# A convolution operand loaded ready-made from four masked copies in HBM, in place of GpSimd copies on chip

## The chip, the cores and the metric

The kernel runs on one core of a Trainium2 chip. The metric is the device time of one execution in microseconds. The core's engines are TensorE (PE; its weight loads are listed as PEld), VectorE (DVE), ScalarE (ACT), GpSimd (POOL) and SyncE (SP), which here issues nearly all DMAs from one queue in order.

## The reference

Two independent computations fill the two halves of one output of 2048 x 1280 (bf16). S is 2048 and D is 640.

```python
# A: gated long convolution
k_shift = sum over t of k_pad[:, t:t+S, :] * shift_k[:, 3-t]     # 4 taps
kv  = k_shift * v
y   = irfft(rfft(kv padded to 2S) * rfft(ssm_k padded to 2S))[:S]  # causal conv per channel
a   = q * (y + kv * ssm_D)
# B: attention with 32 heads of 20
q, k, v = split(x @ wqkv)
b   = softmax(q @ k.T * 20**-0.5) @ v  -> merged heads @ wo
out = concatenate([a, b], axis=-1)
```

The exponentials of B are 32 x 2048 x 2048, which is 2048 tiles of 128 x 512.

## The kernel before

**B.** For each of 4 query chunks of 512, 8 groups of 4 heads and 16 key blocks of 128, four score matmuls (L559) write PSUM banks. ACT takes them two or three banks at a time through Exp into `P_sb` (L576). Some tiles go to DVE instead: a bit-trick exponential in five steps, L606 (reads PSUM), L609, L611, L614 and L616 (writes `P_sb`), in slots of their own. L637 multiplies `P_sb` with V and accumulates over the key blocks in one bank. The casts of K, Q, V and of the results are on DVE. When PE has nothing to do, `zeros` (L314) issues matmuls with a zero operand.

**A, kv stage.** `kv_iter` (L469) builds kv on DVE, 16 blocks of 128 time steps: four products with the taps, three sums, one product with v, each a `tensor_tensor` over 128 x 640 (L472). Each block is stored twice from SP: to `kv_scratch` in order, and to `kvr_scratch` with each run of 32 rows reversed. Two input buffers (`kst`) are loaded two blocks ahead.

**A, convolution.** The causal convolution is a product with Toeplitz tiles. Four channels share one matmul over 128 partitions, each in 32 of them. `hk_load` (L827) brings, for each quad of channels, overlapping rows of the filter from `kext_scratch` into one of four `HK` buffers: four DMAs of 132 KB. The other operand must be block-diagonal: of the four columns of a quad, column X is nonzero only in partitions 32X to 32X+31. `kvr_load` brings half of the channels into `KVr`; `kvx_build` (L833) spreads eight quads of it into one of two `KVX` buffers by four POOL copies of 32 x 512 (L839). The zeros in `KVX` come from two memsets at the start (L816). Inside a `KVX` buffer the 64 columns that a matmul reads are contiguous. `conv_iter` issues 32 matmuls per quad (L871, 8 to 128 columns), for 160 quads; after four quads (16 channels) DVE splits a half of the result into high and low parts (L884, L885), four matmuls add it shifted (L892), and L898 copies the 16 channels into `Y`.

**A, output.** When 20 such groups of 16 channels, thus 320 channels, are done, `A_iter` runs: per block of 128 time steps three DVE steps of 128 x 320 (L914), loads of q and kv and a store (L925) on SP.

**The order** of everything is made while the program is built. A list planner (`Prog`, and the loop from L1078) keeps an estimated time for each engine, with given costs `c` and a DMA estimate of 215 KB per us (L149), and emits each instruction into its engine's fixed stream. It gives ACT its next tiles first; it places conv matmuls and casts in the PE slack that remains; kv and A steps are `micro` work that fills DVE gaps. `vec_at` (L1062) decides whether one more tile goes to DVE: not while kv is behind `(now - 60) * KVPACE` steps, and not while the running `A_iter` is behind its pace of 48 steps per 240 us, or per 60 us once the conv is over. Semaphore waits follow from the buffers (`Buf`); on the chip each engine runs its stream in that order whatever the real times are.

```python
def kvx_build(c):
    B, cl = divmod(c, 10)
    i = c % 2
    for X in range(4):
        dst = sub(KVX[i], [[256, 8], [64, 4], [4, 16]], X, 32 * X, 32)
        src = sub(KVr, [[1, 8], [80, 4], [320, 16]], cl * 8, 32 * X, 32)
```

Of the kernel before, what the change touches and what calls it, by code (L numbers as in the profile page):

```python
# [6 lines left out]
ALU = mybir.AluOpType  # L7
# [4 lines left out]
S = 2048  # L12
D = 640
# [11 lines left out]
NHK = 4  # L25
NPA, NPV = 25, 4
# [4 lines left out]
KVPACE, CONV0, CONVE = 1.0, 560, 40  # L31
# [179 lines left out]
def build_kernel(nc, A_q, A_k, A_v, A_shift_k, A_ssm_k, A_ssm_D, B_x, B_wqkv, B_wo, out):  # L211
# [3 lines left out]
    with ExitStack() as es:  # L215
# [21 lines left out]
        XZ_sb = sb("XZ", [128, 2, 512], FP32)  # L237
# [3 lines left out]
        ident = sb("ident", [128, 128])  # L241
        Win = sb("Win", [128, 128])
        Wc = sb("Wc", [128, 128])
# [3 lines left out]
        HK_E, KVR_E, KVX_E, Y_E, AST_E = HKW, 64 * 80, 8 * 256, 16 * 320, 320  # L247
        ph0 = NCC * 2 * D + 4 * 4 * D + 2 * 5 * D + KS * D + 2 * D + 2 * D
        ph1 = NHK * HK_E + KVR_E + 2 * KVX_E + 2 * Y_E + 5 * AST_E
# [5 lines left out]
        def carve(n):  # L255
# [8 lines left out]
        tA, tB = carve(D), carve(D)  # L264
        kvst = [carve(D) for _ in range(2)]
        pos[0] = 0
        HK = [carve(HK_E) for _ in range(NHK)]
        KVr = carve(KVR_E).rearrange("p (j c) -> p j c", j=64)
        KVX = [carve(KVX_E) for _ in range(2)]
        Y = [carve(Y_E).rearrange("p (t c) -> p t c", t=16) for _ in range(2)]  # L270
        Aq = [carve(AST_E) for _ in range(3)]
        Akv = [carve(AST_E) for _ in range(2)]
# [9 lines left out]
        kvr_d = nc.dram_tensor("kvr_scratch", (S, D), BF16).ap()  # L282

        b_ident, b_Win, b_Wc, b_ones, b_tA, b_tB, b_C = (Buf() for _ in range(7))
# [5 lines left out]
        b_XI, b_XZ = [Buf(), Buf()], [Buf(), Buf()]  # L290
# [10 lines left out]
        b_kvd, b_kext, b_kshT = [], Buf(), Buf()  # L301


        P.op("pool", lambda e: e.memset(ident, 0.0), writes=[b_ident])
        P.op("pool", lambda e: e.affine_select(out=ident, in_=ident, compare_op=ALU.not_equal, fill=1.0, base=0,
                                               pattern=[[-1, 128]], channel_multiplier=1),
# [150 lines left out]
        d_kvr, d_sk, d_kext, d_small = DS("kvr"), DS("sk"), DS("kext"), DS("small")  # L457
# [11 lines left out]
        def kv_iter():  # L469

            def mul(o, a, b, op, reads, writes):
                P.op("dve", lambda e: e.tensor_tensor(o, a, b, op), reads=reads, writes=writes, c=0.49)  # L472

            for j in range(KS):
                src = ap(kst[1], [list(kst[1].ap[0]), [KS, D]], KS - 1 - j)
                yield [b_kst[1]]
                P.op("dve", lambda e, j=j, src=src: e.tensor_copy(Ctile[:, j, :], src), reads=[b_kst[1]], writes=[b_C],
                     c=0.49)
            kst_load(1)
            for tb in range(NKB):  # L480
                i = tb % 2
                k = kst[i]
                yield [b_kst[i]]
                mul(tA, k[:, 0, :], Ctile[:, 0, :], ALU.mult, [b_kst[i], b_C], [b_tA])
                for j in range(1, KS):
                    yield []
                    mul(tB, k[:, j, :], Ctile[:, j, :], ALU.mult, [b_kst[i], b_C], [b_tB])
                    yield []
                    mul(tA, tA, tB, ALU.add, [b_tA, b_tB], [b_tA])
                yield b_kvst[i].r and [RB(b_kvst[i])]  # L490
                mul(kvst[i], tA, k[:, KS, :], ALU.mult, [b_kst[i], b_tA], [b_kvst[i]])
                bd = Buf()
                P.dmas("sp", [(kvd[tb * 128:(tb + 1) * 128, :], kvst[i]),
                              (ap(kvr_d, [[32 * D, 4], [-D, 32], [1, D]], (tb * 128 + 31) * D), kvst[i])], d_kvst[i],
                       reads=[b_kvst[i]], writes=[bd])
                b_kvd.append(bd)
                if tb + 2 < NKB:
                    kst_load(tb + 2)

        def setup_pool():  # L500
            P.op("pool", lambda e: e.memset(V_sb[:, :, :, DH:DH + 1], 1.0), writes=[b_ones])
            for t in (Win, Wc):
                bb = b_Win if t is Win else b_Wc
                P.op("pool", lambda e, t=t: e.memset(t, 0.0), writes=[bb])
                base = 32 if t is Win else -96
                P.op("pool", lambda e, t=t, base=base: e.affine_select(
                    out=t, in_=t, compare_op=ALU.not_equal, fill=1.0, base=base,
                    pattern=[[-1, 128]], channel_multiplier=1), reads=[bb], writes=[bb])
            P.op("pool", lambda e: e.memset(kst[0][0:KS - 1, 0:KS, :], 0.0), writes=[b_kst[0]])
            P.op("pool", lambda e: e.memset(tB, 0.0), writes=[b_tB])  # L510
# [80 lines left out]
        def vexp_iter(n, bk):  # L591
# [4 lines left out]
            XI, XZ, bi, bz = XI_sb[:, i, :], XZ_sb[:, i, :], b_XI[i], b_XZ[i]  # L596
# [206 lines left out]
        d_aq = [DS("aq%d" % i) for i in range(3)]  # L803
        d_ao = [DS("ao%d" % i) for i in range(3)]

        def conv_setup():
            allx = [b_WK0, b_WQ0, b_Wa, b_Wb] + b_x0 + b_xst + b_kst + [b_C, b_tA, b_tB] + b_kvst
            cv["HK"] = [Buf(*allx) for _ in range(NHK)]
            cv["KVr"] = Buf(*allx)
            cv["KVX"] = [Buf(*allx) for _ in range(2)]  # L810
            cv["Y"] = [Buf(*allx) for _ in range(2)]
            cv["Aq"] = [Buf(*allx) for _ in range(3)]
            cv["Akv"] = [Buf(*allx) for _ in range(2)]
            cv["Z"] = [Buf(), Buf()]
            for i in range(2):
                P.op("pool", lambda e, i=i: e.memset(KVX[i], 0.0), writes=[cv["KVX"][i]], c=1.9)  # L816
            kvr_load(0)
            for qd in range(NHK):
                hk_load(qd)
            kvx_build(0)  # L820
            kvx_build(1)

        def kvr_load(B):
            P.dmas("sp", [(KVr[32 * X:32 * X + 32], ap(kvr_d, [[D, 32], [32 * D, 64], [1, 80]], 320 * B + 80 * X))
                          for X in range(4)], d_kvr, reads=b_kvd, writes=[cv["KVr"]])

        def hk_load(qd):  # L827
            B, m = divmod(qd, 80)
            P.dmas("sp", [(HK[qd % NHK][32 * X:32 * X + 32],
                           ap(kext, [[1, 32], [1, HKW]], (320 * B + 80 * X + m) * KXL + 1)) for X in range(4)],  # L830
                   d_hk[qd % NHK], reads=[b_kext], writes=[cv["HK"][qd % NHK]])

        def kvx_build(c):  # L833
            B, cl = divmod(c, 10)
            i = c % 2
            for X in range(4):
                dst = sub(KVX[i], [[256, 8], [64, 4], [4, 16]], X, 32 * X, 32)
                src = sub(KVr, [[1, 8], [80, 4], [320, 16]], cl * 8, 32 * X, 32)
                P.op("pool", lambda e, dst=dst, src=src: e.tensor_copy(dst, src), reads=[cv["KVr"]],  # L839
                     writes=[cv["KVX"][i]] if X == 3 else [], extra=(cv["KVX"][i].r + cv["KVX"][i].w) if X == 0 else (), c=1.35)  # L840
            if cl == 9 and B == 0:
                kvr_load(1)

        def conv_reads(bt):
            rd = []
            for qd in range(4 * bt, 4 * bt + 2):
                rd += [cv["HK"][qd % NHK], cv["KVX"][(qd // 8) % 2]]
            return rd

        def conv_iter():  # L850

            for bt in range(40):
                B, j = divmod(bt, 20)
                for u in range(4):
                    conv_at[0] = u
                    qd = bt * 4 + u
                    c, ql = divmod(qd, 8)
                    i = c % 2
                    slot = qd % NHK
                    for d in range(16):  # L860
                        for r1 in range(2):
# [4 lines left out]
                            rhs = sub(KVX[i], [[64, 2], [1, n]], ql * 256 + r1 * 128)  # L866
# [3 lines left out]
                            yield (cost, [cv["HK"][slot], cv["KVX"][i]] if first else [])  # L870
                            P.op("pe", lambda e, o=o, lhsT=lhsT, rhs=rhs, st=st, last=last: e.matmul(  # L871
                                o, lhsT, rhs, start=st, stop=last, skip_group_check=True),
                                reads=[cv["HK"][slot], cv["KVX"][i]], writes=[bkb[MISC]], tok=last, c=cost,
                                st=0.8 * cost)
                            if last:
                                if qd + NHK < 160:
                                    hk_load(qd + NHK)
                                if ql == 7 and c + 2 < 20:
                                    kvx_build(c + 2)
# [15 lines left out]
                P.op("pe", pe, reads=[bz[0], bz[1], b_Win, b_Wc], writes=[bkb[MISC]], c=0.43, st=0.42)  # L895
# [349 lines left out]
```

## Time and profile before

| What | Value |
|---|---|
| median of 6 runs | 923.43 us (921.43 to 935.74) |
| profiled execution | 925.29 us, span 923.5 us |
| ACT busy | 890.5 us (96%) |
| PE busy | 883.6 us (96%), of which L314 106.7 |
| DVE busy | 631.1 us (68%) |
| POOL busy | 128.0 us (14%) |
| mean granted TensorE clock | 0.985 |
| tiles whose exponential is on DVE (L606) | 110 of 2048 |
| DMA packets | 82015, 129.18 MB |

A row of the groups gives line, engine, operation, tiles, shapes and count, then busy time and mean duration, then the engine's idle time just before and what ended it. In the slices, the span is cut into 40 equal parts of 23.1 us and a digit is the busy share in tenths. PE's ends are modelled, so its busy time is not a measure of how full it is.

### The profile page before, as it was taken

The page shows a single profiled execution, that of the slowest core. Times are in us where ns is not written, and L with a number is a line of the kernel's source. Part 1 is how long each engine was busy: PE and PEld are TensorE (multiplying, and loading weights), DVE is VectorE, ACT ScalarE, POOL GpSimd, SP SyncE. Part 2 cuts the span into 40 slices and gives each one's busy share as a digit, 9 for nine tenths or more (in the row PEclk, how much of TensorE's full clock was granted, in tenths as well). Part 3 has the DMA queues.
Part 4 walks back from the last instruction along what each step waited for, and adds up shares of the span by engine and source line. Part 5 has one row for each costly group of instructions (what it writes and reads, how often), then busy time and mean ns, then how long its engine had stood idle before and what let it go on. Part 6 is the DMA issues. An engine that isn't in the chain of part 4 may idle for free.

```text
span 923.5 us, 26598 instructions
## 1 busy us (share of the span) xinstructions
PE 883.6 (96%) x11742; PEld 413.1 (45%) x11742; DVE 631.1 (68%) x1166; ACT 890.5 (96%) x787; POOL 128.0 (14%) x97
## 2 busy tenths in 40 slices
PE   9999998998988999999999999999999999999998
PEld 5443322223644555555445555555555555422222
DVE  4467666668776777877777778777777776744651
ACT  7999999999997999999999999999999999999995
POOL 3000000006202202222022201222210220000000
PEclk9999999999997999999999999999999999999997
DMA  9421334529644565765586666675675766222000
GB/s 289 160 87 52 124 127 146 165 71 176 170 114 126 150 172 130 188 164 146 146 159 169 162 178 188 173 200 156 173 200 143 188 175 176 70 72 72 12 1 29
DMA packets 82015, 129.18 MB, mean 140 GB/s; under 512 B 32977, under 2 KB 58699, under 8 KB 81899
## 3 DMA queue, kind: packets, MB, share of 16 engines
q1 hardware_dynamic: 79739, 124.36, 49.8%
q0 software_dynamic: 704, 2.74, 0.9%
q8 instruction: 92, 1.51, 0.7%
q10 hardware_dynamic: 1456, 0.37, 0.2%
q14 instruction: 24, 0.20, 0.1%
HBM read 116.81 MB, written 13.23 MB: 141 GB/s over the span
## 4 chain that ended last, share of the span: by engine, by line
PE 52%; ACT 41%; DVE 6%; DMA 1%; issue 0%; SPq 0%; DVEq 0%
ACT P_sb L576 41%; PE PS L871 18%; PE PS L559 14%; PE PS L637 9%; PE PS L389 3%; PE PS L314 2%; PE PS L892 2%; PE PS L711 2%; DVE P_sb L616 2%; DMA R<-in_B_x_dram 1%; DVE XI L614 1%; PE PS L661 1%; DVE XZ L609 1%; PE PS L694 0%; PE PS L740 0%; DVE XZ L611 0%
## 5 line engine op out<-in xcount | busy, mean ns | idle before, releaser
L576 ACT ACTIVATE P_sb<-PS 128x1024 bf16<-128x1024 f32 (+1 forms) x779 | 886.0, 1296 | 19.4 <-PE PS L559 17.5
L559 PE MATMUL PS<-QT,KT 20*128 20x512 bf16 x2048 | 304.7, 388 | 21.4 <-ACT P_sb L576 19.8
L871 PE MATMUL PS<-R 128*128 128x128 bf16 (+15 forms) x5120 | 242.0, 194 | 1.1 <-DVE R L898 0.6
L871 PEld LDWEIGHTS PS<-R 128*128 128x128 bf16 x5120 | 197.9, 97 | 93.4 <-issue 92.9
L839 POOL COPY R<-R 32x512 bf16<-32x512 bf16 x80 | 115.6, 1445 | 423.7 <-PE PS L871 413.6
L559 PEld LDWEIGHTS PS<-QT,KT 20*128 20x128 bf16 x2048 | 74.4, 91 | 218.8 <-ACT P_sb L576 151.0
L637 PE MATMUL PS<-P_sb,V_sb 128*21 128x512 bf16 x2048 | 162.3, 391 | 10.1 <-DVE P_sb L616 10.0
L606 DVE TENSOR_SCALAR XI<-PS 128x512 int32<-128x512 f32 x110 | 76.0, 691 | 110.9 <-PE PS L559 110.5
L314 PE MATMUL PS<-Zt 128*128 128x512 bf16 x358 | 106.7, 393 | 1.0 <-DVE Zt L308 1.0
L616 DVE SCALAR_TENSOR_TENSOR P_sb<-XZ,XI 128x512 uint16<-128x512 f32 x110 | 83.3, 757 | 2.2
L609 DVE SCALAR_TENSOR_TENSOR XZ<-XI 128x512 f32<-128x512 uint16 x110 | 80.5, 732 | 1.2
L611 DVE SCALAR_TENSOR_TENSOR XZ<-XZ,XI 128x512 f32<-128x512 f32 x110 | 79.5, 723 | 2.2
L637 PEld LDWEIGHTS PS<-P_sb,V_sb 128*21 128x21 bf16 x2048 | 33.0, 90 | 73.4 <-issue 48.9
L472 DVE TENSOR_TENSOR R<-R 128x640 bf16<-128x640 bf16 x128 | 61.2, 488 | 5.2 <-DMA R<-in_A_v_dram 1.9
L614 DVE TENSOR_SCALAR XI<-XI 128x512 int16<-128x512 int16 x110 | 58.7, 534 | 2.4
L646 DVE CAST OT_sb<-PS 128x512 bf16<-128x512 f32 x32 | 22.0, 688 | 37.3 <-PE PS L637 37.0
L314 PEld LDWEIGHTS PS<-Zt 128*128 128x128 bf16 x358 | 23.9, 98 | 40.3 <-issue 33.1
L389 PE MATMUL PS<-xT,R 128*20 128x512 bf16 (+2 forms) x660 | 40.4, 374 | 0.0
L389 PE MATMUL PS<-xT,WQ 128*20 128x512 bf16 (+1 forms) x660 | 40.2, 374 | 0.0
L377 DVE CAST KT<-PS 128x512 bf16<-128x512 f32 (+1 forms) x32 | 21.7, 679 | 26.2 <-PE PS L389 26.2
L450 DVE CAST V_sb<-PS 128x160 bf16<-128x160 f32 (+1 forms) x48 | 18.4, 382 | 21.6 <-PE PS L444 20.8
L377 DVE CAST QT<-PS 128x512 bf16<-128x512 f32 (+1 forms) x32 | 21.9, 683 | 16.0 <-PE PS L389 15.7
(56 smaller groups left out, 354.9 us busy)
## 6 DMA issues: line engine op xcount, KB each, us to landing
R<-kext_scratch SPq DMA_DIRECT2D x640, 132.0 KB, 3.0
R<-in_A_k_dram SPq DMA_DIRECT2D x15, 640.0 KB, 3.9
kext_scratch<-in_A_ssm_k_dram POOLq DMA_DIRECT2D x1, 2560.0 KB, 14.3
R<-in_A_v_dram SPq DMA_DIRECT2D x16, 160.0 KB, 5.4
kv_scratch<-R SPq DMA_DIRECT2D x16, 160.0 KB
kvr_scratch<-R SPq DMA_DIRECT2D x16, 160.0 KB
R<-kvr_scratch SPq DMA_DIRECT2D x8, 320.0 KB, 6.5
R<-in_A_q_dram SPq DMA_DIRECT2D x32, 80.0 KB, 2.2
```

Of the source, the lines that this page charges most:

```text
L314: P.op("pe", lambda e: e.matmul(bank[bk], Zt, zrhs, start=start, stop=start, skip_group_check=True), reads=[b_Zt], writes=[bkb[bk]], tok=s ...
L389: ins = e.matmul(bank[bk][32 * i:32 * i + DH, 0:n], Wt[:, cc, off + i * DH:off + (i + 1) * DH], xT[:, cc, x0:x0 + n], start=(cc == 0), sto ...
L559: ins = e.matmul(bank[b], KT[32 * u:32 * u + DH, g, kb * 128:(kb + 1) * 128], QT[32 * u:32 * u + DH, qs(qc, g), :], start=True, stop=True, ...
L576: P.op("act", lambda e: e.activation(P_sb[:, s0:s0 + k, :], PS[:, b0 * 512:(b0 + k) * 512].rearrange("p (u q) -> p u q", u=k), ACT.Exp, sc ...
L606: step(lambda e: e.tensor_scalar(XI, bank[bk], scale * 1.4426950408889634 * w, 127.0 * w, op0=ALU.mult, op1=ALU.add), [bkb[bk]], [bi])
L609: step(lambda e: e.scalar_tensor_tensor(XZ, u, w * c2 / c3, u, op0=ALU.add, op1=ALU.mult), [bi], [bz])
L611: step(lambda e: e.scalar_tensor_tensor(XZ, XZ, w * w * c1 / c3, u, op0=ALU.add, op1=ALU.mult), [bi, bz], [bz])
L614: step(lambda e: e.tensor_scalar(hi, hi, 128.0, None, op0=ALU.mult), [bi], [bi])
L616: step(lambda e: e.scalar_tensor_tensor(P_sb[:, slot[n], :].bitcast(U16), XZ, 128.0 * c3 / w ** 3, hi, op0=ALU.mult, op1=ALU.add), [bi, bz ...
L637: ins = e.matmul(bank[OBANK][32 * u:32 * u + DH + 1, :], V_sb[:, kb, 4 * g + u, :], P_sb[:, slot[4 * b + u], :], start=(kb == 0), stop=(kb ...
L839: P.op("pool", lambda e, dst=dst, src=src: e.tensor_copy(dst, src), reads=[cv["KVr"]], writes=[cv["KVX"][i]] if X == 3 else [], extra=(cv[ ...
L871: P.op("pe", lambda e, o=o, lhsT=lhsT, rhs=rhs, st=st, last=last: e.matmul(o, lhsT, rhs, start=st, stop=last, skip_group_check=True), read ...
```

## The change

`kv_iter` computes two taps in one instruction and stores kv in order once. In addition DVE copies each kv block into one of two tiles `KM`, at every fifth group of positions, such that copy X of the four in a tile holds only the channels with index X modulo 4 and is zero elsewhere. Four DMAs per block store these to `kvm_scratch`, each run of 32 rows reversed. `KVr`, the POOL copies and the memsets of `KVX` are gone; two DVE memsets clear `KM`. `kvx_load` brings 128 channels at once into `KVX`, one DMA for each X, in pieces of 128 channels (256 B); the next chunk's four loads are issued after each of the first four groups of 16 channels of the present one. The matmuls (before L871) read their columns from `KVX` at a step of 128 channels per 32 time steps, four adjacent elements at a time. `A_iter` runs five times, once per 128 channels, in four steps of 512 time steps, with two `Aq` buffers instead of three. Its pace becomes 12 steps per 60 us, or per 20 us once the conv is over; KVPACE becomes 0.9. The second exponential path has one `XZ` buffer instead of two. `ident`, `Win` and `Wc` become windows of one tile. The `HK` buffers wait only for what lay in their own memory.

```diff
+CH = 128
-KVPACE, CONV0, CONVE = 1.0, 560, 40
+KVPACE, CONV0, CONVE = 0.9, 560, 40
...
-        XZ_sb = sb("XZ", [128, 2, 512], FP32)
+        XZ = sb("XZ", [128, 512], FP32)
...
+            for i in range(2):
+                yield [RB(b_xst[2 + i])]
+                b_KM.append(Buf(b_xst[2 + i]))
+                P.op("dve", lambda e, i=i: e.memset(KM[i], 0.0), writes=[b_KM[i]], c=0.8)
...
-                yield [b_kst[i]]
-                mul(tA, k[:, 0, :], Ctile[:, 0, :], ALU.mult, [b_kst[i], b_C], [b_tA])
+                for j in range(0, KS, 2):
+                    yield [b_kst[i]]
+                    mul(tB[:, j:j + 2, :], k[:, j:j + 2, :], Ctile[:, j:j + 2, :], ALU.mult, [b_kst[i], b_C], [b_tB], 0.82)
                 for j in range(1, KS):
                     yield []
-                    mul(tB, k[:, j, :], Ctile[:, j, :], ALU.mult, [b_kst[i], b_C], [b_tB])
-                    yield []
-                    mul(tA, tA, tB, ALU.add, [b_tA, b_tB], [b_tA])
+                    mul(tA, tA if j > 1 else tB[:, 0, :], tB[:, j, :], ALU.add, [b_tA, b_tB], [b_tA])
...
-                P.dmas("sp", [(kvd[tb * 128:(tb + 1) * 128, :], kvst[i]),
-                              (ap(kvr_d, [[32 * D, 4], [-D, 32], [1, D]], (tb * 128 + 31) * D), kvst[i])], d_kvst[i],
-                       reads=[b_kvst[i]], writes=[bd])
                 if tb + 2 < NKB:
                     kst_load(tb + 2)
+                P.dma("sp", kvd[tb * 128:(tb + 1) * 128, :], kvst[i], d_kvst[i], reads=[b_kvst[i]], writes=[bd])
+                yield b_KM[i].r and [RB(b_KM[i])]
+                P.op("dve", lambda e, i=i: e.tensor_copy(sub(KM[i], [[D + 1, 4], [4, D // 4]]),
+                                                         sub(kvst[i], [[1, 4], [4, D // 4]])),
+                     reads=[b_kvst[i]], writes=[b_KM[i]], c=0.73)
+                P.dmas("sp", [(ap(kvm_d, [[32 * D, 4], [-D, 32], [1, D]], (X * S + tb * 128 + 31) * D),
+                               KM[i][:, X * D:(X + 1) * D]) for X in range(4)], d_km[i], reads=[b_KM[i]], writes=[bm])
...
-            for i in range(2):
-                P.op("pool", lambda e, i=i: e.memset(KVX[i], 0.0), writes=[cv["KVX"][i]], c=1.9)
-            kvr_load(0)
-            for qd in range(NHK):
+            hk_load(0)
+            for X in range(4):
+                kvx_load(0, X)
+            for qd in range(1, NHK):
                 hk_load(qd)
-            kvx_build(0)
-            kvx_build(1)
...
+        def kvx_load(c, X):
+            P.dma("sp", KVX[c % 2][32 * X:32 * X + 32].rearrange("p (j c) -> p j c", j=64),
+                  ap(kvm_d, [[D, 32], [32 * D, 64], [1, CH]], X * S * D + CH * c), d_kvx[c % 2][X],
+                  reads=b_kvm, writes=[cv["KVX"][c % 2][X]])
...
-                            rhs = sub(KVX[i], [[64, 2], [1, n]], ql * 256 + r1 * 128)
+                            rhs = sub(KVX[i], [[CH, 2], [4 * CH, 16 - d], [1, 4]], r1 * 2 * CH + 4 * ql)
...
-                                if ql == 7 and c + 2 < 20:
-                                    kvx_build(c + 2)
+                                if u == 3 and j < 4 and c + 1 < D // CH:
+                                    kvx_load(c + 1, j)
...
-            for tp in range(16):
+            for h in range(4):
...
-                P.dma("sp", ap(out2, [[2 * D, 128], [1, 320]], tp * 128 * 2 * D + 320 * B), Aq[i], d_ao[i], reads=[q])
+                P.dma("sp", ap(out2, [[2 * D, 128], [128 * 2 * D, 4], [1, CH]], h * 512 * 2 * D + CH * B), Aq[i],
+                      d_ao[i], reads=[q])
...
-            elif micro and kv_done[0] < a_at[0] + 48 * (now - a_at[1]) / (60 if conv_over else 240):
+            elif micro and kv_done[0] < a_at[0] + 12 * (now - a_at[1]) / (20 if conv_over else 60):
```

## The prediction

> **What bounds the kernel.** I read the slices first, then the groups, then busy times by stage, then the waits of the convolution stage, and last the timeline of one disturbed place. From the slices, ScalarE (ACT), GpSimd (POOL) and the granted TensorE clock:
>
> ```profile
> ACT  7999999999997999999999999999999999999995
> POOL 3000000006202202222022201222210220000000
> PEclk9999999999997999999999999999999999999997
> ```
>
> ACT is full nearly everywhere; the one hole inside the run (slice 13, 277 to 300 us) has POOL at work and a lowered clock. ACT does the exponentials (L576: 575.4 + 432.3 us in the two shapes), so the time is ACT's work plus ACT's idle time. By stage (columns: stretch, length, PE, PEld, DVE, ACT, POOL busy with counts, clock, DMA share, GB/s):
>
> ```profile
> 60.00:208.00 148.00, 138.14 (x1447) 43.77 (x1444) 98.27 (x199) 147.91 (x132) 0.00 (x0) 1.00 0.35 114
> 208.00:320.00 112.00, 103.61 (x1435) 52.80 (x1432) 82.80 (x135) 102.66 (x90) 29.93 (x20) 0.92 0.62 149
> 320.00:440.00 120.00, 117.55 (x1843) 64.83 (x1844) 91.83 (x153) 118.35 (x105) 26.24 (x19) 1.00 0.59 159
> 440.00:560.00 120.00, 117.25 (x1778) 63.02 (x1774) 90.08 (x161) 119.31 (x106) 23.03 (x16) 1.00 0.65 163
> 560.00:680.00 120.00, 119.21 (x1897) 65.26 (x1893) 91.64 (x168) 119.53 (x106) 23.17 (x16) 1.00 0.67 179
> 680.00:800.00 120.00, 118.46 (x1857) 66.26 (x1853) 88.37 (x162) 118.21 (x103) 17.03 (x12) 1.00 0.63 166
> ```
>
> Before 208 us ACT idles 0.09 us in 148. From 208 to 800 us it works 102.66 + 118.35 + 119.31 + 119.53 + 118.21 = 578.06 of 592 us: 13.9 us idle, and POOL works only there. The waits of 208 to 800 us (total, times, longest) and one place of the timeline (start, length) show the path:
>
> ```profile
> PEld PS L559 <- ACT P_sb L576: 48.2, 122, 0.8
> PEld PS L637 <- DVE P_sb L616: 15.9, 21, 2.7
> ACT P_sb L576 <- PE PS L559: 12.3, 18, 2.1
> ```
>
> ```profile
> 284.72 3.32 POOL L839 COPY R<-R 32x512 bf16<-32x512 bf16 x2
> ...
> 285.40 1.47 DVE L614 TENSOR_SCALAR XI<-XI 128x512 int16<-128x512 int16 x1
> ...
> 286.90 1.45 DVE L616 SCALAR_TENSOR_TENSOR P_sb<-XZ,XI 128x512 uint16<-128x512 f32 x1
> ...
> 288.40 0.61 PE L637 MATMUL PS<-P_sb,V_sb 128*21 128x512 bf16 x4 [2.44 <-DVE P_sb L616]
> ...
> 289.60 2.36 ACT L576 ACTIVATE P_sb<-PS 128x1536 bf16<-128x1536 f32 x2 [2.07 <-PE PS L559]
> ```
>
> While a POOL copy runs, VectorE (DVE) steps of the second exponential path stretch: L614 takes 1.47 us where its median is 0.458, L616 1.45 where it is 0.691. L637, fixed in PE's order, waits 2.44 us, the next scores come late, ACT idles 2.07. L606, which reads PSUM, never exceeds 0.694 us.
>
> **Removed.** L839's 80 copies of 1445 ns (115.6 us) and L816's two memsets (3.8 us) leave POOL. POOL bounds nothing; what counts is ACT's idle time behind them. Mean over median times 110 gives the DVE time lost beside the copies: L609 5.3, L611 3.5, L614 8.4, L616 7.3, together 24.4 us, reaching ACT as at most 13.9. Some is ordinary PE jitter: I take the 12.3 us of ACT waits less what lies outside copies, **-12.0** (0 to -13.9; the lower end if another wait stands right behind).
>
> **The kv stage on DVE.** L472 costs 488 ns at 640 elements, L914 326 ns at 320: 0.506 ns an element, so a double-width product (1280) costs 0.812 us. After: 32 x 0.812 + 48 x 0.488 + 16 x 0.488 = 57.2 us, where L472 has 61.2. The masked copy (640 elements at step 4) has a near row, L477, a copy reading at step 4: 0.497 us. Bounds 0.5 and 1.0; I take 0.6, 9.6 us for 16. Two memsets, about 2. Sum +7.6 us. The 50 us in which DVE idles from 60 to 208 us hide it; without this cover kv ends 8 us later, the conv starts later and about two DVE exponentials are lost. One moved from DVE to ACT costs 1514 - 1088 = 0.43 us. I take **+0.4** (0 to +1.0). Two plain stores per block become one plain and four masked ones on SP's queue; behind them stand only later kv loads, and loads for block tb+2 are now issued ahead of both. DMA moves 114 GB/s at a share of 0.35 there; 0.64 MB of masked stores every 9 us add some 71 GB/s, a share near 0.6.
>
> **Start of the conv.** Once the last masked store has landed, one Toeplitz tile (hk) and then four loads of 2048 pieces of 256 B (2.10 MB) must arrive. The row for that is the old load of 8192 pieces of 160 B (1.31 MB):
>
> ```profile
> 208.23 5.35 SPq L190 DMA_DIRECT2D R<-kvr_scratch  x4
> 218.35 12.21 POOL L839 COPY R<-R 32x512 bf16<-32x512 bf16 x8 [6.31 <-DMA R<-kvr_scratch]
> ```
>
> 10.1 us from issue to first use: the same piece count gives 10.1, the same byte rate 16.2. The Trainium skill (DMA: Bandwidth & Descriptors, Why small descriptors are slow) prices 256 B at 11 cycles, which at its 850 MHz over 16 engines is an estimate of 8192 x 12.9 ns / 16 = 6.6 us; the measured row is slower, and I stay with it. The planner, at its 215 KB/us plus 2.2 us, expects 12.0. PE could stand at L871 for -1.9 to +4.2 us beyond plan; I take **+1.0** (0 to +4). By the page's price it would be 0.
>
> **Later loads.** Four chunks each bring four kvx loads on SP, one per 16 channels. An hk tile is asked for three tiles ahead: 160 tiles in 575 us is 3.6 us each, 10.8 us of lead, of which four issues of 0.42 and a landing of 3.0 use 4.7. A kvx load takes 1.8 us of issue and 2.5 to 4.0 of transfer; it fits in the remaining 6.1. The old 1.31 MB load at 467 us went out in one piece with ACT busy 20.00 of 20 us. Cost 0. With two Aq buffers in place of three, SP waits for an output store to land (1.9 us) before the next A load, with hk loads queued behind: also inside the 6.1. If both fall together, half a microsecond.
>
> **A output.** 96 DVE steps of 32.3 us become 60 of 326 + 192 x 0.506 = 423 ns, 25.4 us: 20.3 instead of 16.2 inside the conv, 5.1 instead of 15.2 after it. A DVE exponential takes 0.691 + 0.684 + 0.691 + 0.458 + 0.691 = 3.2 us: the conv loses 1.3 of them, **+0.5**. After 800 us the pace rule for A held them back: two start before 850 us, eight in the 35 us from 852. With twelve A steps left instead of 48 I take five more, **-2.1** (0 to -3.4). The planner sees neither POOL's interference nor the strided read.
>
> **The conv's moving operand.** It now reads pieces of four elements, 1 KB apart, in place of runs of 64. No row has that; the nearest are the conv itself:
>
> ```profile
> L871 PE MATMUL PS<-R 128*128 128x128 bf16 x320 | 48.0, 220 | 1.1 <-DVE R L898 0.6 <-POOL R L839 0.4
> L871 PE MATMUL PS<-R 128*128 128x8 bf16 x320 | 31.7, 167 | 0.0
> ```
>
> 53 ns for 120 columns is 0.44 ns each. Against the change speaks the Trainium skill (SBUF — State Buffer, the note on cachelines under Door 1): each move to a new 16-byte line pays, unless a line is hit at least twice. Four elements are four hits, so by its letter 0. No run here shows it. A conv tile has 2176 columns, 160 tiles 348,160 columns, 87,040 pieces: one cycle of about 0.42 ns a piece is +36 us of PE, and half rate 348,160 x 0.44 = +153 us. A gain is excluded[...]. I take 0 and keep the +36 for a rival.
>
> **Sum.** -12.0 + 0.4 + 1.0 + 0.5 - 2.1 = -12.2 us. The profiled execution took 925.29 us (span 923.5, 1.8 around it), so 913.1; it lay 1.9 above the median of 923.43, so **911.2 us**. Its own range, with the ends above, is 906 to 917.
>
> **Rivals.** Differences within 0.5% (4.6 us) are about what a measurement of this kernel can't tell from none.
> 1. As summed, 911.2 us: chance 0.60.
> 2. Slower, by one mechanism: each piece of the moving operand costs PE a cycle. PE waits 48.2 us for ACT in that stage, so about half of 36 us is absorbed: 911.2 + 18 = 929 us; at half rate 153 - 48 = +105, 1016 us. It decides once a piece costs over 0.28 ns (24 us of PE, half of them felt, eats the 12 us). For: 1 KB steps. Against: the four hits per line. Chance 0.17.
> 3. A transfer wait replaces the POOL stall: 4 us at the start and half a microsecond at each of 16 kvx loads, +12: 923 us (917 to 930). For: DMA share already 0.6 to 0.8 in the stage. Against: 467 us. Chance 0.15.
> 4. The change frees POOL but ACT's idle time stays, since the static order stands behind DVE anyway: -2.1 and +1.9, 923 us. Against: no idle time before 208 us. Chance 0.08.
>
> Faster: 0.60 plus 0.03 of the third, 0.63; same: 0.06 and 0.07 of the third and fourth, 0.13; slower: 0.17, 0.06 and 0.01, 0.24. The range reaches from 905 to 930, through the third and fourth cases and up to the mild end of the second.
>
> **What would show it.** Right: no L839; maxima of L609 to L616 below 0.75 us; ACT idle below 3 us from conv start to conv end; clock 1.00 in slice 13; L871 still 220 ns at 128 columns; 112 to 118 DVE exponentials. Wrong: L871 at 250 ns or more; waits of L871 for kext_scratch or kvm_scratch; L606 below 105.

## The result, and the profile after

The changed kernel takes 920.34 us (median of 30 executions, 917.86 to 931.58) against 925.89 us for the kernel before (65 executions): ratio 0.9952, interval 0.9936 to 0.9968. Ratios, here and below, leave out executions more than 1.5% above the fastest of their kernel. The sign of the forecast holds, but the gain is 5.6 us where 12.2 were forecast: 920.34 us lies inside the range of 905 to 930, outside the 906 to 917 given for the sum, and far from 911.2. The profiled execution took 919.81 us (span 918.0). Executions of either kernel scatter by some 14 us, for the most part with the granted clock of TensorE (last section).

The slices of the profile after. POOL has gone after the first 23 us, and the hole in ACT's row has moved: from slice 13 (277 to 300 us, before) to slices 8 and 9 (about 160 to 207 us), and the lowered clock went with it.

```profile
ACT  6999999879999999999999999999999999999996
POOL 3000000000000000000000000000000000000000
PEclk9999999889999999999999999999999999999999
```

Busy times by stage, after (same columns as in the prediction: stretch, length, PE, PEld, DVE, ACT, POOL, clock, DMA share, GB/s):

```profile
140.00:226.00 86.00, 74.89 (x696) 19.86 (x697) 53.04 (x87) 75.80 (x68) 0.00 (x0) 0.90 0.48 167
226.00:320.00 94.00, 92.15 (x1359) 48.57 (x1358) 69.53 (x125) 93.65 (x84) 0.00 (x0) 1.00 0.85 201
320.00:440.00 120.00, 117.38 (x1828) 62.26 (x1827) 83.50 (x152) 118.82 (x106) 0.00 (x0) 1.00 0.71 177
440.00:560.00 120.00, 118.37 (x1810) 64.29 (x1809) 84.13 (x155) 119.34 (x106) 0.00 (x0) 1.00 0.72 182
560.00:680.00 120.00, 118.80 (x1815) 62.20 (x1815) 86.62 (x158) 119.64 (x105) 0.00 (x0) 1.00 0.73 184
680.00:800.00 120.00, 119.22 (x1842) 67.05 (x1834) 86.46 (x161) 119.76 (x106) 0.00 (x0) 1.00 0.68 180
```

ACT is the bound in both kernels, so the account is made in ACT's idle time, length less busy time, over the whole span:

| ACT idle, us | 0 to 60 | 60 to 226 | 226 to 800 | 800 to the end | sum | ACT busy | span |
|---|---|---|---|---|---|---|---|
| before | 8.0 | 0.4 | 13.6 | 10.9 | 33.0 | 890.5 | 923.5 |
| after | 8.9 | 10.2 | 2.8 | 7.6 | 29.5 | 888.5 | 918.0 |

The conv stage gives up 10.8 us, near the forecast. But 9.8 us of new idle time stand in the stage before it, the kv stage, which had almost none. The waits of 60 to 226 us after (total, times, longest) name it:

```profile
DVE R L505 <- DMA kvm_scratch<-R: 15.6, 7, 3.4
ACT P_sb L582 <- PE PS L565: 10.0, 8, 2.4
DVE R L475 <- DMA R<-in_A_v_dram: 6.7, 7, 1.4
```

L505 is the masked copy. There are two `KM` tiles, so it waits until the masked stores of the block before last have landed. L475 (the products, L472 before) waits for a kv load that stands behind those stores on SP's queue. The SP timeline of one block, and the DMA share while little but stores runs (timeline: start, length; window: as above):

```profile
159.73 0.43 SPq L191 DMA_DIRECT2D kv_scratch<-R  x1
160.21 6.32 SPq L191 DMA_DIRECT2D kvm_scratch<-R  x4
166.57 1.73 SPq L191 DMA_DIRECT2D R<-in_A_k_dram  x1
168.35 0.43 SPq L191 DMA_DIRECT2D R<-in_A_v_dram  x1
168.82 1.48 SPq L191 DMA_DIRECT2D kv_scratch<-R  x1
170.34 5.41 SPq L191 DMA_DIRECT2D kvm_scratch<-R  x4
```

```profile
166.00:168.00 2.00, 2.00 (x15) 0.45 (x17) 0.98 (x2) 1.46 (x3) 0.00 (x0) 0.50 0.25 95
208.00:210.00 2.00, 1.84 (x29) 0.63 (x31) 1.15 (x3) 1.96 (x2) 0.00 (x0) 1.00 0.27 98
```

Four stores of 160 KB hold SP's queue for 5.4 to 6.3 us, and from 160 us on the queue is full back to back. The DMA share goes with it: 0.25 to 0.27 of 16 engines, as much as four busy engines would give, at 95 to 98 GB/s; 655 KB at 98 GB/s are 6.7 us. The store's destination is four runs of 32 rows, each run backwards: `[[32 * D, 4], [-D, 32], [1, D]]`.

How that reaches ACT is in the timeline of one such place:

```profile
192.75 0.90 DVE L505 COPY R<-R 128x640 bf16<-128x640 bf16 x1 [3.37 <-DMA kvm_scratch<-R]
...
196.24 0.68 DVE L652 CAST OT_sb<-PS 128x512 bf16<-128x512 f32 x1
...
196.98 0.40 PE L667 MATMUL PS<-shifts,OT_sb 128*128 128x128 bf16 x4 [3.17 <-DVE OT_sb L652]
...
197.83 1.02 ACT L582 ACTIVATE P_sb<-PS 128x1024 bf16<-128x1024 f32 x1 [2.37 <-PE PS L565]
```

L505 waits 3.37 us at the head of DVE's fixed stream. Queued behind it, after another cast and two products, is the cast L652, so PE's L667 comes 3.17 us late and the next scores L565 with it, and ACT idles 2.37 us. After PE's gap the granted clock is 0.50 until 206 us. PE is then the slower engine, and ACT loses more:

```profile
198.00:200.00 2.00, 2.00 (x20) 0.56 (x20) 0.98 (x3) 0.85 (x1) 0.00 (x0) 0.50 0.66 239
```

### The profile page after: what moved, and what is told of

It is laid out like the page before. It is cut to its first block, busy times and chain, and to the rows that moved or that the text cites. A ratio compares the mean times of both kernels' runs of the same rounds, so it can differ in the third digit from the quotient of the medians.

```text
span 918.0 us, 26512 instructions
## 1 busy us (share of the span) xinstructions
PE 883.1 (96%) x11758; PEld 412.1 (45%) x11758; DVE 625.9 (68%) x1131; ACT 888.5 (97%) x786; POOL 7.8 (1%) x11
## 4 chain that ended last, share of the span: by engine, by line
PE 49%; ACT 43%; DMA 4%; DVE 3%; SPq 1%; issue 0%; DVEq 0%
ACT P_sb L582 43%; PE PS L866 16%; PE PS L565 13%; PE PS L643 8%; PE PS L391 4%; PE PS L316 3%; DMA R<-in_A_v_dram 3%; PE PS L887 1%; SPq L191 1%; PE PS L717 1%; DMA kvm_scratch<-R 1%; DVE R L475 1%; PE PS L667 0%; PE PS L700 0%; PE PS L746 0%
## 5 line engine op out<-in xcount | busy, mean ns | idle before, releaser
L565 PE MATMUL PS<-QT,KT 20*128 20x512 bf16 x2048 | 303.5, 387 | 21.1 <-ACT P_sb L582 18.9
L866 PE MATMUL PS<-R 128*128 128x128 bf16 (+15 forms) x5120 | 240.6, 193 | 1.5 <-DVE R L893 1.4
L866 PEld LDWEIGHTS PS<-R 128*128 128x128 bf16 x5120 | 196.4, 96 | 93.8 <-issue 93.3
L565 PEld LDWEIGHTS PS<-QT,KT 20*128 20x128 bf16 x2048 | 74.5, 91 | 224.1 <-ACT P_sb L582 158.1
L643 PE MATMUL PS<-P_sb,V_sb 128*21 128x512 bf16 x2048 | 157.9, 385 | 1.9 <-DVE P_sb L622 1.9
L612 DVE TENSOR_SCALAR XI<-PS 128x512 int32<-128x512 f32 x113 | 78.2, 692 | 112.0 <-PE PS L565 111.6
L316 PE MATMUL PS<-Zt 128*128 128x512 bf16 x374 | 110.1, 392 | 1.0 <-DVE Zt L310 1.0
L615 DVE SCALAR_TENSOR_TENSOR XZ<-XI 128x512 f32<-128x512 uint16 x113 | 78.0, 690 | 3.1
L617 DVE SCALAR_TENSOR_TENSOR XZ<-XZ,XI 128x512 f32<-128x512 f32 x113 | 77.7, 688 | 2.3
L622 DVE SCALAR_TENSOR_TENSOR P_sb<-XZ,XI 128x512 uint16<-128x512 f32 x113 | 77.7, 687 | 2.1
L475 DVE TENSOR_TENSOR R<-R 128x640 bf16<-128x640 bf16 (+1 forms) x96 | 57.7, 601 | 8.5 <-DMA R<-in_A_v_dram 6.7
L643 PEld LDWEIGHTS PS<-P_sb,V_sb 128*21 128x21 bf16 x2048 | 31.3, 89 | 59.4 <-issue 47.1
L620 DVE TENSOR_SCALAR XI<-XI 128x512 int16<-128x512 int16 x113 | 51.7, 457 | 2.3
L391 PE MATMUL PS<-xT,R 128*20 128x512 bf16 (+2 forms) x660 | 42.5, 389 | 0.0
L652 DVE CAST OT_sb<-PS 128x512 bf16<-128x512 f32 x32 | 22.0, 689 | 26.0 <-PE PS L643 25.9
L446 PE MATMUL PS<-R,xT 128*128 128x160 bf16 (+1 forms) x240 | 28.9, 256 | 0.1
## 6 DMA issues: line engine op xcount, KB each, us to landing
kext_scratch<-in_A_ssm_k_dram POOLq DMA_DIRECT2D x1, 2560.0 KB, 13.6
```

The source lines that it names most:

```text
L316: P.op("pe", lambda e: e.matmul(bank[bk], Zt, zrhs, start=start, stop=start, skip_group_check=True), reads=[b_Zt], writes=[bkb[bk]], tok=s ...
L391: ins = e.matmul(bank[bk][32 * i:32 * i + DH, 0:n], Wt[:, cc, off + i * DH:off + (i + 1) * DH], xT[:, cc, x0:x0 + n], start=(cc == 0), sto ...
L565: ins = e.matmul(bank[b], KT[32 * u:32 * u + DH, g, kb * 128:(kb + 1) * 128], QT[32 * u:32 * u + DH, qs(qc, g), :], start=True, stop=True, ...
L612: step(lambda e: e.tensor_scalar(XI, bank[bk], scale * 1.4426950408889634 * w, 127.0 * w, op0=ALU.mult, op1=ALU.add), [bkb[bk]], [bi])
L615: step(lambda e: e.scalar_tensor_tensor(XZ, u, w * c2 / c3, u, op0=ALU.add, op1=ALU.mult), [bi], [bz])
L617: step(lambda e: e.scalar_tensor_tensor(XZ, XZ, w * w * c1 / c3, u, op0=ALU.add, op1=ALU.mult), [bi, bz], [bz])
```

## The experiments

Seven kernels, against two theories. **Stores:** the idle time of the kv stage comes from the masked stores alone, which run on four DMA engines because of their four runs; everything else in the forecast stands. **Rivals:** the estimates of the planner put the block too early; the added DVE work is the cause; or removing the POOL copies is worth less than 12 us to begin with.

**Is the POOL stall worth what was forecast?** The kernel before, with each of the 80 copies cut down to one element per partition. It leaves out filling the operand of the convolution; the order is that of before.

```diff
-                dst = sub(KVX[i], [[256, 8], [64, 4], [4, 16]], X, 32 * X, 32)
-                src = sub(KVr, [[1, 8], [80, 4], [320, 16]], cl * 8, 32 * X, 32)
+                dst = sub(KVX[i], [[1, 1]], X, 32 * X, 32)
+                src = sub(KVr, [[1, 1]], cl * 8, 32 * X, 32)
```

> The kernel before, with each of the 80 POOL copies cut to one element per partition, at the same places and with the same waits; it leaves out the filling of the convolution's operand. The order on all engines is that of before. If the stalls of the conv stage are the copies' interference with DVE: ACT idle from 208 to 800 us falls from 13.9 to under 3 us, L614 and L616 stay under 0.75 us, the time falls by 10 to 13 us to 911 to 914. If the static order would stand anyway: ACT idle above 10 us, about 923.

Measured: 909.75 us against 925.97 for the kernel before beside it, ratio 0.9834 (0.9787 to 0.9881), span 908.8. ACT's idle time of 226 to 800 us falls from 13.6 to 4.1 us. So in all the copies cost about 16 us. L609, L611 and L616 stay under 0.70 us; one L614 step of 1.53 us stands beside the memset L816 on POOL, which this version keeps. Not all of the gain is in the conv stage. Of 14.7 us between the two profiled executions 9.5 are idle time there, 2.9 are idle time after 800 us (in before the clock is at 0.50 from 900 to 908 us) and 2.4 are ACT's busy time. Whether these two lie at the copies' door can't be told from one profile each.

**The stores alone.** The kernel before, its one reversed store per block done four times into four regions, of which three are read by nobody. No DVE instruction is added, and the planner counts two stores as before, so the order stays.

```diff
...
-                              (ap(kvr_d, [[32 * D, 4], [-D, 32], [1, D]], (tb * 128 + 31) * D), kvst[i])], d_kvst[i],
-                       reads=[b_kvst[i]], writes=[bd])
+                              *((ap(kvr_d, [[32 * D, 4], [-D, 32], [1, D]], (X * S + tb * 128 + 31) * D), kvst[i])
+                                for X in range(4))], d_kvst[i], reads=[b_kvst[i]], writes=[bd], n=2)
...
```

> The kernel before, with its store of a kv block to kvr_scratch done four times, to four places, three of them read by nobody; the order on every engine is that of before. Theory A: five stores of a block take 6 to 7 us of SP, the kv stage becomes bound by the DMA queue, DVE's last product of a block (L472) waits for the store two blocks back, ACT idle from 60 to 226 us rises from 0.4 to between 5 and 12 us, 5 to 12 us above before. If the stall of the kernel after comes from its DVE work alone: no change.

Measured: 944.08 us against 923.94, ratio 1.0195 (1.0143 to 1.0247). The waits of 60 to 226 us in it, and two windows:

```profile
DVE R L472 <- DMA R<-in_A_v_dram: 30.9, 11, 5.0
ACT P_sb L576 <- PE PS L559: 14.3, 7, 4.2
```

```profile
161.00:163.00 2.00, 1.61 (x21) 0.30 (x13) 0.00 (x0) 2.00 (x3) 0.00 (x0) 1.00 0.26 102
163.00:165.00 2.00, 0.39 (x2) 0.09 (x2) 1.30 (x3) 2.00 (x2) 0.00 (x0) 1.00 0.26 97
165.00:167.00 2.00, 0.66 (x5) 0.56 (x6) 1.70 (x5) 0.23 (x1) 0.00 (x0) 0.77 0.94 308
```

ACT idles 14.4 us in 60 to 226 us, where before has 0.4, with no work added to DVE: the stores are enough. The effect is larger than the 5 to 12 us expected, though SP issues the four stores of a block in 2.2 to 4.2 us where 6 to 7 were expected for all five. It also comes by another wait: the loads are issued behind the stores here, so DVE waits for v and not for the store two blocks back. The share of 0.26 goes to 0.94 when the loads behind the stores come through (third row).

**The stores in another pattern.** The kernel after, its masked stores in plain row order, which is 128 runs. It leaves out the reversal of 32 rows; the same bytes move, and loads and order are unchanged.

```diff
-                P.dmas("sp", [(ap(kvm_d, [[32 * D, 4], [-D, 32], [1, D]], (X * S + tb * 128 + 31) * D),
+                P.dmas("sp", [(ap(kvm_d, [[D, 128], [1, D]], (X * S + tb * 128) * D),
```

> The kernel after, with the four masked stores of a block written in plain row order, 128 runs instead of 4, and the kvx loads unchanged; it leaves out the reversal of the 32 rows, so the convolution gets its rows in the wrong order. Bytes, pieces and the order on every engine are unchanged. Theory A (four engines only): a block's stores take 2 to 2.7 us, no waits of L505, ACT idle from 60 to 226 us near 0 and, since the loads are those of the kernel after, no wait of L866 at the conv start either: 910 to 912, 8 to 10 us below the kernel after. Theory D (with faster stores the kv stage ends some 12 us earlier and the conv start meets the kvx load anyway, as with 8 runs): a wait of L866 of 2 to 4 us and a half clock behind it, 915 to 921.

Measured: 908.70 us against 923.94, ratio 0.9834 (0.9784 to 0.9883), span 905.9, clock 1.00. The SP timeline of a block, a window in which hardly anything but stores moves, and busy times from the kv stage on:

```profile
163.04 2.59 SPq L191 DMA_DIRECT2D kvm_scratch<-R  x4
```

```profile
166.00:167.00 1.00, 0.59 (x9) 0.21 (x10) 0.93 (x3) 1.00 (x2) 0.00 (x0) 1.00 1.10 397
```

```profile
140.00:226.00 86.00, 78.38 (x789) 22.19 (x781) 59.86 (x100) 85.98 (x77) 0.00 (x0) 1.00 0.68 191
226.00:320.00 94.00, 92.67 (x1461) 52.15 (x1459) 68.44 (x123) 93.61 (x83) 0.00 (x0) 1.00 0.70 182
320.00:440.00 120.00, 117.10 (x1816) 62.23 (x1814) 85.19 (x155) 118.82 (x105) 0.00 (x0) 1.00 0.72 184
```

The same bytes are issued in 1.8 to 2.6 us and leave at 397 GB/s. (A share adds up the times of packets and can pass 1.) L505 waits for no store, ACT idles 0.03 us between 60 and 226 us, and the conv rows are those of after to a few hundredths of a microsecond. Between this run and after the span differs by 12.1 us: 10.2 of ACT idle time in the kv stage, 0.8 before 60 us, 1.2 of ACT busy time. The pattern of the stores accounts for the missing gain. The block's DVE work and its bytes are those of after, so neither is the cause by itself. This edit changes the number of runs and the reversal together; that the reversal isn't the cause is shown by the run with eight reversed runs below.

**The stores from another queue.** The kernel after, complete, its four reversed stores issued from POOL instead of SP.

```diff
-                P.dmas("sp", [(ap(kvm_d, [[32 * D, 4], [-D, 32], [1, D]], (X * S + tb * 128 + 31) * D),
+                P.dmas("pool", [(ap(kvm_d, [[32 * D, 4], [-D, 32], [1, D]], (X * S + tb * 128 + 31) * D),
```

> The kernel after, with the four masked stores issued from POOL's queue instead of SP's, same patterns; the order on PE, DVE and ACT is unchanged. If POOL's stores of 4 runs go to different DMA engines, a block's stores overlap and take under 3 us, L505 waits little: 910 to 914. If they go to the same four, as from SP: L505 waits as in the kernel after, but kv loads no longer stand behind them on SP, so the waits of L475 fall: 917 to 920. If writing the descriptors on POOL interferes with DVE: L475 and L505 stretch, 925 or more.

Measured: 910.10 us against 923.94, ratio 0.9844 (0.9797 to 0.9892), span 905.9. From the timeline of POOL, a window with these stores alone, the waits of 60 to 226 us, and the time from issue to landing (size, median us), here and in the run with plain rows:

```profile
163.01 2.73 POOL L191 DMA_DIRECT2D kvm_scratch<-R  x4 [8.65 <-DVE R L505]
```

```profile
167.00:169.00 2.00, 2.00 (x33) 0.58 (x31) 1.46 (x4) 2.00 (x3) 0.00 (x0) 1.00 0.61 144
```

```profile
DVE R L505 <- DMA kvm_scratch<-R: 4.0, 3, 3.1
```

```profile
kvm_scratch<-R POOLq DMA_DIRECT2D x64, 160.0 KB, 5.8
kvm_scratch<-R SPq DMA_DIRECT2D x64, 160.0 KB, 3.8
```

The four stores of a block, unchanged in pattern, now reach a share of 0.61 and 144 GB/s, more than four engines would give, and no load stands behind them on SP. They are not as quick as expected, 5.8 us to landing and not under 3. It is enough all the same: L505 waits 4.0 us in place of 15.6, L475 1.1 us for v in place of 6.7, and ACT idles 0.03 us from 60 to 226 us. POOL is busy 2.73 us per block with issuing, and DVE doesn't feel it: L505 takes 883 ns here, 886 in after. The run changes the engines and the queue at once; that the pattern alone is enough is shown by the run with plain rows. This version leaves nothing out, and it is faster than both kernels.

**More runs on SP's queue.** Stores of 8 runs of 16 rows, or of 16 runs of 8. The rows then lie in another order in HBM, so each load for the conv is split into two, or four, over 16 or 8 partitions.

```diff
-                P.dmas("sp", [(ap(kvm_d, [[32 * D, 4], [-D, 32], [1, D]], (X * S + tb * 128 + 31) * D),
+                P.dmas("sp", [(ap(kvm_d, [[16 * D, 8], [-D, 16], [1, D]], (X * S + tb * 128 + 15) * D),
...
-            P.dma("sp", KVX[c % 2][32 * X:32 * X + 32].rearrange("p (j c) -> p j c", j=64),
-                  ap(kvm_d, [[D, 32], [32 * D, 64], [1, CH]], X * S * D + CH * c), d_kvx[c % 2][X],
-                  reads=b_kvm, writes=[cv["KVX"][c % 2][X]])
+            P.dmas("sp", [(KVX[c % 2][32 * X + 16 * h:32 * X + 16 * h + 16].rearrange("p (j c) -> p j c", j=64),
+                           ap(kvm_d, [[D, 16], [32 * D, 64], [1, CH]], (X * S + 16 * (1 - h)) * D + CH * c)) for h in range(2)],
+                   d_kvx[c % 2][X], reads=b_kvm, writes=[cv["KVX"][c % 2][X]])
```

> The kernel after, with the masked stores cut as 8 runs of 16 reversed rows instead of 4 runs of 32, and each kvx load as two loads of 16 partitions; the order on PE, DVE, ACT and POOL is unchanged, the bytes and pieces too. Theory A (a store whose outermost run count is 4 is spread over 4 of the 16 DMA engines, so a block's four stores take 6.2 us and the kv stage waits for the DMA queue): four stores take 3 to 3.5 us, DMA share while they run alone near 0.5 instead of 0.27, waits of L505 for the stores fall from 15.6 to under 2 us, ACT idle from 60 to 220 us from 13 to under 2 us, the time falls by 8 to 10 us against the kernel after, to about 911. Theory B (writes of 1280 B rows to HBM, or the volume in the queue, set the rate): stores stay at 6 us, waits of L505 at 15 us, about 920. Theory C (the DVE work added to kv, the masked copy at 0.88 us above all, holds up the casts by itself): no change, about 920.

> As the one with 8 runs, but the stores cut as 16 runs of 8 reversed rows, and each kvx load as four loads of 8 partitions. Theory A: four stores in about 2 us or what issuing them takes, DMA share near 1 while they run, time equal to the version with 8 runs within 1.5 us, about 911; the loads of 8 partitions could give back up to 2 us at the start of the conv. Theories B and C: about 920.

Measured: 921.89 us with eight runs (ratio 0.9947, 0.9924 to 0.9971), 968.64 with sixteen (six executions, 951.11 to 977.30; ratio 1.0343, 1.0244 to 1.0441, from two of them), against 925.97. About 911 was expected for both. In both the kv stage is clean, with ACT idle for 0.03 to 0.04 us from 60 to 226 us. With eight runs, still reversed, the stores of a block are issued in 2.4 to 3.5 us, and alone they move twice what four runs do:

```profile
168.00:169.00 1.00, 1.00 (x22) 0.39 (x20) 0.75 (x2) 1.00 (x2) 0.00 (x0) 1.00 0.53 196
```

The gain is given back from the start of the conv on. The SP timeline and the wait of L866 (L871 before), eight and then sixteen:

```profile
211.13 14.16 SPq L191 DMA_DIRECT2D R<-kvm_scratch  x8
...
231.42 0.66 PE L866 MATMUL PS<-R 128*128 128x128 bf16 x5 [3.79 <-DMA R<-kvm_scratch]
```

```profile
209.97 28.44 SPq L191 DMA_DIRECT2D R<-kvm_scratch  x16
...
244.96 0.27 PE L866 MATMUL PS<-R 128*128 128x128 bf16 x1 [18.49 <-DMA R<-kvm_scratch]
```

The same 2.1 MB take 6.5 us of issue in after, 14.2 and 28.4 us here. PE then stands 3.8 or 18.5 us in its fixed order, half clock follows, and with eight runs ACT idles 6.8 us in 226 to 320 and 4.7 us in 320 to 440 us (this second loss is not followed up here). These two runs confirm the cause of the kv stage's stall, but show nothing on the total, since the edit brought a wait of its own.

**Only the planner's estimate.** The kernel after, the planner told that the masked stores take 2.1 times as long.

```diff
-                               KM[i][:, X * D:(X + 1) * D]) for X in range(4)], d_km[i], reads=[b_KM[i]], writes=[bm])
+                               KM[i][:, X * D:(X + 1) * D]) for X in range(4)], d_km[i], reads=[b_KM[i]], writes=[bm], slow=2.1)
...
```

> The kernel after, with only the planner's estimate of the four masked stores raised by 2.1 (to the 6.2 us that they take); the stores themselves are unchanged, the order of the instructions from the kv stage on is another. Theory A: the masked copies are placed when their tile is really free, waits of L505 for the stores fall under 3 us and ACT idle from 60 to 220 us under 3 us; the kv stage ends no earlier (220 us) and one to four fewer tiles go to DVE; 911 to 915. Theory C: no change, about 920.

Measured: 921.88 us, ratio 0.9945 (0.9921 to 0.9969). The blocks are spaced wider and the idle time of 60 to 226 us is gone (0.03 us), so the stall is one of a schedule that doesn't know the rate of these stores. The 911 to 915 us expected did not come. By the time alone this run would speak for the rival, which had foretold about 920; it is the waits that decide. The new order has its own stall later.

```profile
351.03 0.40 PE L643 MATMUL PS<-P_sb,V_sb 128*21 128x512 bf16 x4 [1.40 <-DVE P_sb L622]
```

```profile
320.00:440.00 120.00, 113.58 (x1618) 57.97 (x1615) 78.50 (x143) 110.80 (x98) 0.00 (x0) 0.91 0.61 154
```

ACT idles 9.2 us in this stretch. L612 at 349.69 us waited 1.93 us for its scores, the last step L622 of another tile stands behind it in DVE's stream, and the PV product then waits 1.40 us for L622; half clock follows, 0.53 to 0.65 from 350 to 366 us. With 103 exponentials on DVE in place of 113, ten more fall to ACT, some 4.3 us at the 0.43 us of the prediction (ACT's busy time is 3.8 us longer). So spacing the blocks wider had its price; the run with plain rows has no such stall (ACT idles 1.2 us in this stretch).

## Why the prediction was half right

**What bounds the kernel**: right. ACT's busy time is 887.3 to 892.9 us in all nine profiles, while the spans go from 905.9 to 970.1 us: they differ mostly by ACT's idle time.

**POOL's copies, -12.0**: right in place and mechanism. No DVE step of the second exponential path exceeds 0.70 us any more (means: L615 690 ns, L617 688, L620 457, L622 687), ACT idles 2.8 us from the start of the conv to 800 us, below the 3 us named, and the clock is 1.00. From 208 to 800 us that is 11.1 us less than before. Taken alone, with the copies cut down, the term measured -16.2 in time, of which 9.7 are ACT's idle time in this stretch.

**The kv stage, +0.4 (0 to +1.0)**: wrong; this is the step that failed, and it measured +9.8. Its DVE half did no harm: the double-width product takes 825 ns where 812 were worked out, the masked copy 886 where I took 600, 4.6 us more over 16 blocks, and all of it is hidden in the run with plain rows. What failed is the sentence on the masked stores: "behind them stand only later kv loads" and "DMA moves 114 GB/s at a share of 0.35 there; 0.64 MB of masked stores every 9 us add some 71 GB/s, a share near 0.6". It priced the stores as bytes spread evenly over 16 engines. They reach the rate of four, so a block holds SP's queue for about 6 us plus 3 us of loads and stores; that is 9.1 us from block to block (160.21, 170.34, 178.38, 187.47, 196.50), where the same order takes 6 to 7 if the stores let it (163.04, 169.67, 175.79 in the run with plain rows). An estimate from the sizes: four engines that carry the masked stores and a quarter of the block's other transfers (655 KB of k, 164 of v, 164 of plain store) have 901 KB to move, at 98 GB/s 9.2 us. Both the loads and the free `KM` tile come late, and "the 50 us in which DVE idles" hide nothing, because DVE's stream is fixed and what waits at its head holds the casts behind it.

The kernel before showed it in its own windows. Its reversed store has the same pattern with a quarter of the bytes, and follows a plain store of the same block (SP timeline of before; then a window in which the plain store leaves, and one in which the reversed store is alone):

```profile
196.23 0.33 SPq L190 DMA_DIRECT2D kv_scratch<-R  x1
196.60 0.52 SPq L190 DMA_DIRECT2D kvr_scratch<-R  x1
```

```profile
197.00:197.50 0.50, 0.50 (x16) 0.10 (x4) 0.20 (x1) 0.50 (x2) 0.00 (x0) 1.00 0.83 310
198.50:199.50 1.00, 0.93 (x8) 0.21 (x4) 0.93 (x3) 1.00 (x2) 0.00 (x0) 1.00 0.27 100
```

The second row is the one that four times as many bytes should have been priced by: 655 KB at 100 GB/s are 6.6 us a block and 105 us for 16, not "a share near 0.6". The Trainium skill has the rule behind it (DMA: Bandwidth & Descriptors, Why a DMA increments its semaphore by 16 and not by 1, the paragraph on how many engines): a DMA uses the largest number of engines up to 16 that divides the outermost size on both sides, the lowest-numbered ones when it comes from a hardware queue, and consecutive ones from a moving start when from GpSimd's. With 4 runs on the one side and 128 partitions on the other that is 4, and four such stores in a row on SP take the same four. The runs agree at each point that they show, in windows with hardly anything but the stores: share 0.25 to 0.27 and 95 to 100 GB/s for four runs on SP, 0.53 and 196 for eight, 1.10 and 397 for 128 rows, 0.61 and 144 for four runs issued from POOL. Which engines they were isn't in the views read here.

**Start of the conv, +1.0**: it was 0. No wait for the kvx loads appears in 208 to 320 us of after, nor in the run with plain rows, where the conv stage starts earlier. The four loads took 6.5 us of issue, near the 6.6 us that the prediction worked out and set aside for a row of 10.1. The runs with split loads show how near a wait lay: at 14.2 us of issue PE waits 3.8.

**Later loads, 0**: right; ACT idles 2.4 us in the 480 us from 320 to 800.

**A output and the tail, +0.5 and -2.1**: right in sum. A steps take 422 ns (423 worked out); 113 tiles are on DVE against 110, within 112 to 118: 17 instead of 10 after 800 us, 95 instead of 97 from 208 to 800. Three tiles fewer on ACT are 1.3 us at 0.43; ACT's busy time is 2.0 lower. No term of the sum held two other differences between the profiles: ACT idles 3.3 us less after 800 us and 0.9 us more before 60 us. Their causes were not looked for; without them the gain would have been smaller still, so here luck helped.

**The strided operand, 0**: right, and with it the slower rival falls. L866 at 128 and at 8 columns, after:

```profile
L866 PE MATMUL PS<-R 128*128 128x128 bf16 x320 | 46.6, 219 | 1.5 <-DVE R L893 1.4
L866 PE MATMUL PS<-R 128*128 128x8 bf16 x320 | 32.1, 167 | 0.0
```

219 and 167 ns where the contiguous operand had 220 and 167: four elements per step of 1 KB cost nothing.

**The rivals.** The third came nearest: a transfer wait in the place of the POOL stall, 923 us (917 to 930). But it put the wait at the loads of the conv; it stands at the stores, one stage earlier. With the stores made faster, the change gives 908.7 to 910.1 us, where 911.2 was forecast. That nearness is in part luck: -16.2 for the copies and some 1 to 2 us the other way for the rest, where the sum had -12.0 and -0.2.

**The range**: the 906 to 917 called "its own range, with the ends above" isn't the sum of these ends. Added up, they reach from 906.6 to 928.9 us, since the copies' own range goes down to no gain at all.

## To carry to other kernels

Price a DMA by the rate that its own pattern reached, not by bytes over the mean of all engines: look for a window in which only such a DMA runs, and read share and GB/s together. Here four runs gave 0.27 and 98 GB/s, eight gave 0.53 and 196. Where the share stays low, what helped here was another outermost size (8 or 128 runs), or issuing the stores from another queue. But look at what the new pattern does to the loads that read it, as the split loads show. And in a stream of fixed order, idle time of an engine covers work that is added to it, but not a wait that is added at its head.

## What the runs showed besides

Half clock is a price of its own. Over 43 executions of the kernel before, the span goes up by 0.78 us for each microsecond's worth of clock lost (913.3 us where the line meets full clock), thus some 0.39 us for each microsecond spent at 0.50; it is a fit and not an experiment. Each PE wait on L667, L866 and L643 shown above, 1.4 us and longer, was followed by such a stretch, and ACT lost more than the wait's own length (5.0 us of idle time from 196 to 206 us after the 3.17 us of L667).

Loads of 256 B pieces onto fewer partitions are slower at the same bytes in these runs. Windows inside the loads, onto 32 partitions (the run with plain rows), 16 and 8:

```profile
212.00:214.00 2.00, 1.70 (x15) 0.52 (x12) 1.32 (x3) 2.00 (x3) 0.00 (x0) 1.00 1.27 232
```

```profile
214.00:216.00 2.00, 1.70 (x12) 0.57 (x12) 1.36 (x3) 2.00 (x3) 0.00 (x0) 1.00 1.34 122
```

```profile
214.00:216.00 2.00, 1.96 (x18) 0.44 (x16) 1.93 (x4) 2.00 (x4) 0.00 (x0) 1.00 0.69 64
```

From 16 to 8 partitions the share halves with the rate, which fits half as many engines. From 32 to 16 the rate halves at the same share; the runs don't show why.
